# Decay attention and two expert layers in fp32: right-side tiles at multiples of 64 bytes, block sums on VectorE and spread over items, tiles r and hh elsewhere

## Chip, cores, metric

The kernel runs on one core of a Trainium2 chip. The metric is the device time in microseconds (us) of one execution; lower is better. The kernel before took 885.96 us, the median of three runs (884.93 to 888.58).

## What is computed

```python
scores = (q @ k.T) / 8 + minimum(-(cum[i] - cum[j]), 0)   # causal; cum = cumsum(max(s, 0))
x = softmax(scores) @ v                   # 4 batches, 8 heads, 576 tokens, 64 wide -> x [2304, 512]
h = maximum(x @ w_in, 0)                  # w_in [512, 2048]
x = (h * h) @ w_out                       # w_out [2048, 512]
h = maximum(x @ w1, x @ w2, x @ w3)       # each [512, 768]
out = h @ w_out2                          # [768, 512]
```

All is float32 (the weights come as 64-bit numbers whose bits the kernel takes apart). A matrix product is made of three matmuls on pairs of float32r tiles, a high part and a low part: high by high, high by low, low by high.

## The kernel before, in words

The program has three stages, one behind the other on TensorE (PE). Every engine works through its own queue in the order in which the program was written; the kernel is recorded with a manual schedule, so nothing reorders it.

**Attention** goes over 16 head pairs in 9 units each. Its last steps scale an output tile `ax` by reciprocal row sums `px` on GpSimd (`w_px`, line 795) and store it to `x_at` in HBM (`w_xst`, line 800). The first products of the next stage (`first_products`) are already made between its last units.

**Stage 1** is the first expert layer, in nine visits of token chunks: the three chunks of 512 and one of 384 tokens with the first 8 of 16 feature blocks, the last chunk of 384 with all 16, then the four again with the last 8. An item is one block: 12 matmuls `h` (line 813, moving operand `xs`), then on ScalarE (ACT) relu (line 976), square (977) and the high copy into `hh` (978), on VectorE (DVE) the low part (979), and two items later 12 matmuls `x` (line 999) that stream `hh` as the moving operand into four accumulating PSUM banks. Weights stand in slots `sl` of 4 KB in each partition, 15 of them in the first visit and 19 later, and one more, `slb`, on the right side. The class `Slots` decides what is loaded, made (lines 398 to 439) or fetched back, and evicts the weight whose next use is farthest.

**Stage 2** is the second layer: three groups of 768 tokens, 9 items in each, 7 products of 6 matmuls in each item (line 1139; a block algorithm with 7 products in place of 8). Its operands are sums and differences of four raw tiles `xr` of the input, each split into high and low parts in a tile `xs` by `operand` (ACT line 805, DVE line 808); four of the seven operands need a difference first, made in place by GpSimd (line 928). The results are joined on DVE by `after` (lines 1058, 1075, 1080) into `res`, `split_out` splits `res` into `hh`, and 18 matmuls (line 1111) make each 128 output tokens. In the queue of PE the products of item n and those of item n-1 take turns: (n,0), (n-1,4), (n,1), (n-1,5), (n,2), (n-1,6), (n,3). All operands of the next group are made while a group's last item, number 8, runs:

```python
if m % PER == PER - 1 and g < last:
    ops.pop((g, i))
    operand(g + 1, i)
```

SBUF is handed out from two ends. Left are the slots, the attention's tiles, and `xs`, `xr`; right are the staging tiles `st`, `wa`, `slb` and the tiles `hh`, `r`, `sums`, `hi`, `pt` of stage 1. In the built program every right-side tile of stage 1 starts 32 bytes past a multiple of 64 (`hh` at 190,432, `r` at 164,832), and the left-side ones at a multiple of 64. The two buffers of `r` lie on bytes that `ax` and `px` of the attention used.

Of the kernel before, what the change touches and what calls it, by code (L numbers as in the profile page):

```python
# [17 lines left out]
SLOTS_B = 1  # L18
# [20 lines left out]
RETIRE = 16  # L39
QUIET = 0  # L40
PACE_EARLY = 1.5
# [47 lines left out]
class Slots:  # L89
# [8 lines left out]
    def __init__(self, steps, make, bring, early, room, parts):  # L98
        self.steps = steps
        self.uses = {}  # L100
        for n, ids in enumerate(steps):
            for i in ids:
                self.uses.setdefault(i, []).append(n)
        self.make, self.bring, self.early, self.room = make, bring, early, dict(room)
        self.parts = parts
        self.free = []
        self.retired = []
        self.held = {}
        self.open = []
        self.kept = set()  # L110
        self.coming = set()
        self.pos = 0
        self.clock = 0.0
        self.last = -100.0
        self.pace = PACE_ATT
        self.phase = 0
        self.soon_kept = SOON_KEPT
        self.most = ADV_ATT
        self.idle = ()
        self.quiet = set()  # L120
# [13 lines left out]
    def evict(self, n):  # L134
        busy = [job.i for job in self.open]
        while True:
            far = max((j for j in self.held if j not in busy), key=self.next_use)
            if self.next_use(far) <= n:
                return False
            t = self.held.pop(far)  # L140
            if not any(t is r for r in self.retired):
                self.free.append(t)
                return True

    def retire(self, tiles):
        self.retired = tiles
        self.free = [t for t in self.free if not any(t is r for r in tiles)]
# [104 lines left out]
def kernel(  # L252
# [57 lines left out]
    phS = ExitStack()  # L310
    stage_p = phS.enter_context(tc.tile_pool(name="stage", bufs=ST_BUFS, side="right"))
    slots_b = phS.enter_context(tc.tile_pool(name="slb", bufs=1, side="right"))
    slots_b = [slots_b.tile([P, 2, 512], F32R, name=f"slb{i}") for i in range(SLOTS_B)]

# [210 lines left out]
    slots.add(slots_a[:-HELD_BACK] + slots_b)  # L525
# [358 lines left out]
    def experts():  # L884
        xs_p = ctx.enter_context(tc.tile_pool(name="xs", bufs=8, reuse_waits="tile"))
        xr_p = ctx.enter_context(tc.tile_pool(name="xr", bufs=4, reuse_waits="tile"))
# [36 lines left out]

        def operand(g, i):
            a, b, c, d = (raw[g, k] for k in range(4))
            sub = {1: (a, b, a), 2: (a, d, a), 4: (b, d, b), 6: (a, c, a)}.get(i)
            if sub:
                nc.gpsimd.tensor_tensor(out=sub[0], in0=sub[1], in1=sub[2], op=ALU.subtract)  # L928
            x = {3: c, 4: b, 5: d}.get(i, a).rearrange("p (k c) -> p k c", c=T2)
            t = ops[g, i] = xs_p.tile([P, 2, 2, T2], F32R, tag="xs", name="xs")  # L930
            high(x, t[:, :, 0, :])
            low_of(x, t[:, :, 0, :], t[:, :, 1, :])

        with ExitStack() as ph1:
            h_p, sp, r_p, pt_p = (ph1.enter_context(tc.tile_pool(name=n, bufs=b, side="right", reuse_waits="tile"))
                                  for n, b in (("hh1", 4), ("spare", 1), ("rr1", RR), ("part", 4)))
# [9 lines left out]
            for kind, v, m, f in main1:  # L946
# [4 lines left out]
                if kind == "h":  # L951
# [9 lines left out]
                    if nxt:  # L961
                        for kk in range(KD):
                            if to_end == 7 - kk:
                                xload(v + 1, *nxt, kk)
                    elif to_end in (7, 6):
                        for i in range(2):
                            raw_load(0, 2 * (7 - to_end) + i)
                    if end:
                        for kk in (2, 3):
                            if nxt:  # L970
                                xs[v + 1, kk] = xsplit(v + 1, nxt[1], kk)
                            else:
                                operand(0, kk)
# [8 lines left out]
                    if to_end in (5, 3):  # L982
# [3 lines left out]
                        else:  # L986
                            operand(0, kk)
# [4 lines left out]
                else:  # L992
                    w = slots.get(("out", f))
                    hh = hs.pop((v, m))
                    for d in range(KD):
# [5 lines left out]
                        if end:  # L1001
# [9 lines left out]
                            nc.sync.dma_start(out=(part if v < last1 else x_mid)[d, :, t0:t0 + n], in_=dst)  # L1011
                slots.pos += 1
                if slots.pos == len(main1) - RETIRE:
                    slots.retire(slots_b)
                slots.pump(n / 512)
            for i in range(4, 7):
                operand(0, i)
# [5 lines left out]
        for i in [i for i, t in slots.held.items() if any(t is b for b in slots_b)]:  # L1023
            del slots.held[i]
        phS.close()
        slots.soon_kept = SOON_KEPT_2
        with ExitStack() as ph2:
            r_p, hh_p, c_p, s_p, o_p = (ph2.enter_context(tc.tile_pool(name=n, bufs=2, reuse_waits="tile"))
                                        for n in ("rr2", "hh2", "cc2", "ss2", "oo2"))
# [95 lines left out]
            for item in main2:  # L1125
                if item[0] == "p":
# [16 lines left out]
                    if m % PER == PER - 1 and g < last:  # L1143
                        ops.pop((g, i))
                        operand(g + 1, i)
                    if m % PER == PER - 1 and i == 6 and g < last:
                        split_out(g, 0, range(NQ))
                    if m == len(items) - 1 and i == 5:
                        for t in range(2):
                            split_out(last, t, order2[:-1])  # L1150
# [74 lines left out]
```

## Time and profile before

| | before |
|---|---|
| median of 3 runs | 885.96 us (884.93 to 888.58) |
| profiled execution, its own time | 887.15 us |
| its span, first to last instruction | 885.4 us |
| PE busy | 842.1 us (95%), 5284 matmuls |
| DVE busy | 536.0 us (61%) |
| ACT busy | 409.7 us (46%) |
| GpSimd (POOL) busy | 180.9 us (20%) |
| granted TensorE clock, mean | 0.992 of full |

The profile is of one execution. Its page gives busy time by engine, the chain of waits that ended last, and groups of instructions by line. "PEclk" is the granted TensorE clock as a share of the full 2.4 GHz; the lower level is 1.2 GHz, 0.5. A busy PE is not a PE at its peak: matmuls overlap, so how fast it goes is read from the starts of rows that follow each other.

### The profile page before, as it was taken

The numbers are of one execution on the slowest core, as the hardware profiler recorded it, in microseconds if no ns is written. First come the engines' busy times: TensorE is split into PE (matmuls) and PEld (weight loads), VectorE is DVE, ScalarE is ACT, GpSimd is POOL, SyncE is SP. The second block draws the span as 40 slices with busy tenths as digits, with TensorE's granted clock in tenths as the row PEclk, the third lists the DMA queues.
The fourth block names the chain that finished last, engine by engine and source line by source line (L and its number), as shares of the span: only waits on it lengthen the run. The fifth ranks groups of instructions, "written<-read, shape, count | busy, mean of one in ns | idle before, by whom it ended". The sixth has DMA issues, their size and how long they took to land.

```text
span 885.4 us, 14354 instructions
## 1 busy us (share of the span) xinstructions
PE 842.1 (95%) x5284; PEld 708.0 (80%) x5284; DVE 536.0 (61%) x1047; ACT 409.7 (46%) x831; POOL 180.9 (20%) x245
## 2 busy tenths in 40 slices
PE   5899899889999999999999999999989999899998
PEld 3555555458888889999998888889988899789986
DVE  6788787938675556656678686644364343733342
ACT  5788878854444444445444544442242212321212
POOL 2042333334111222213123232220030001200000
PEclk9999999999999999999999999999999999999999
DMA  4555567534244654796559586639911572026501
GB/s 136 169 159 173 166 186 196 171 124 142 79 161 136 205 183 144 285 363 225 199 179 312 174 295 227 236 132 405 378 48 42 200 261 92 13 72 227 200 1 71
DMA packets 71925, 158.70 MB, mean 179 GB/s; under 512 B 11312, under 2 KB 31344, under 8 KB 71856
## 3 DMA queue, kind: packets, MB, share of 16 engines
q1 hardware_dynamic: 56916, 107.45, 35.8%
q0 software_dynamic: 14928, 50.34, 16.6%
q8 instruction: 41, 0.67, 0.3%
q14 instruction: 28, 0.23, 0.1%
q10 hardware_dynamic: 12, 0.01, 0.0%
HBM read 112.48 MB, written 45.27 MB: 178 GB/s over the span
## 4 chain that ended last, share of the span: by engine, by line
PE 83%; DVE 7%; ACT 4%; DMA 2%; issue 2%; POOL 1%; SPq 0%; ACTq 0%; DVEq 0%; POOLq 0%
PE banks L999 23%; PE banks L813 11%; PE first L813 11%; PE banks L1139 11%; PE banks L1111 9%; PE first L1139 7%; PE pairs L782 4%; PE pairs L730 3%; PE pair L648 2%; PE pairs L648 2%; DVE e L671 1%; DVE xs L808 1%; ACT et L759 1%; ACT et L757 1%; ACT e L685 1%
## 5 line engine op out<-in xcount | busy, mean ns | idle before, releaser
L999 PE MATMUL banks<-hh,sl 128*128 128x512 f32 (+1 forms) x900 | 203.8, 376 | 2.6 <-ACT hh L978 2.6
L999 PEld LDWEIGHTS banks<-hh,sl 128*128 128x128 f32 x900 | 166.3, 189 | 28.1 <-ACT hh L978 3.0
L1139 PE MATMUL banks<-xs,sl 128*128 128x384 f32 x702 | 133.5, 339 | 4.1 <-DVE c L1058 4.1
L1139 PEld LDWEIGHTS banks<-xs,sl 128*128 128x128 f32 x702 | 124.6, 191 | 5.7 <-DVE c L1058 4.8
L979 DVE TENSOR_TENSOR hh<-r,hh 128x512 fp32r<-128x512 f32 (+1 forms) x80 | 52.3, 653 | 121.6 <-ACT hh L978 121.4
L813 PE MATMUL first<-xs,sl 128*128 128x512 f32 (+1 forms) x432 | 94.7, 368 | 0.0
L813 PE MATMUL banks<-xs,sl 128*128 128x512 f32 (+1 forms) x432 | 94.7, 368 | 0.0
L1139 PE MATMUL first<-xs,sl 128*128 128x384 f32 x432 | 86.1, 338 | 2.9 <-DVE xs L808 2.4
L685 ACT ACTIVATE e<-e,nm 128x128 f32<-128x128 f32 (+2 forms) x144 | 83.4, 582 | 11.3 <-DVE nm L671 11.2
L813 PEld LDWEIGHTS first<-xs,sl 128*128 128x128 f32 x432 | 79.0, 188 | 10.4
L813 PEld LDWEIGHTS banks<-xs,sl 128*128 128x128 f32 x432 | 79.0, 188 | 10.4
L1111 PE MATMUL banks<-sl,hh 128*128 128x512 f32 (+1 forms) x342 | 80.3, 388 | 4.1 <-DVE hh L808 3.7
L1139 PEld LDWEIGHTS first<-xs,sl 128*128 128x128 f32 x432 | 76.6, 190 | 4.2 <-DVE xs L808 3.0
L1111 PEld LDWEIGHTS banks<-sl,hh 128*128 128x128 f32 x342 | 62.4, 191 | 19.0 <-DVE hh L808 6.0
L976 ACT ACTIVATE r<-first 128x512 f32<-128x512 f32 (+1 forms) x40 | 22.2, 556 | 109.9 <-PE first L813 101.6
L976 ACT ACTIVATE r<-banks 128x512 f32<-128x512 f32 (+1 forms) x40 | 22.2, 556 | 92.5 <-PE banks L813 92.5
L730 PEld LDWEIGHTS pairs<-identF,e 64*128 64x128 f32 x800 | 33.5, 139 | 30.8 <-ACT et L759 23.2
L928 POOL TENSOR_TENSOR xr<-xr 128x768 f32<-128x768 f32 x12 | 24.9, 2088 | 162.1 <-DVE xs L808 162.1
L730 PE MATMUL pairs<-identF,e 64*128 64x64 f32 x800 | 41.4, 231 | 17.0 <-ACT et L759 17.0
L1040 ACT COPY s<-first 128x384 f32<-128x384 f32 x36 | 17.2, 479 | 79.5 <-PE first L1139 79.3
L782 PEld LDWEIGHTS pairs<-et,xv 128*64 128x64 f32 (+1 forms) x448 | 27.8, 136 | 31.2 <-ACT e L685 8.9
L782 PE MATMUL pairs<-et,xv 128*64 128x320 f32 (+4 forms) x448 | 52.7, 367 | 0.0
(108 smaller groups left out, 1200.4 us busy)
## 6 DMA issues: line engine op xcount, KB each, us to landing
sl<-keep_p SPq DMA_DIRECT2D x68, 512.0 KB
st<-in_w_dram POOLq DMA_DIRECT2D x36, 256.0 KB, 5.7
st<-in_w_out_dram POOLq DMA_DIRECT2D x35, 256.0 KB, 4.1
sl<-keep_out SPq DMA_DIRECT2D x14, 512.0 KB
keep_p<-hi POOLq DMA_DIRECT2D x9, 768.0 KB, 4.8
keep_p<-sums POOLq DMA_DIRECT2D x9, 768.0 KB, 6.2
xr<-x_at SPq DMA_DIRECT2D x20, 256.0 KB
xk<-in_kT_dram SPq DMA_DIRECT2D x16, 288.0 KB
```

The source lines that it names most:

```text
L648: nc.tensor.matmul(b[:, j, 0:w], lhsT=d["xq"][rows(j), w - P:w], rhs=d["xk"][rows(j), 0:w], start=True, stop=False)
L685: nc.scalar.activation(out=e_u[u][:, 0:w], in_=e_u[u][:, 0:w], func=ACTF.Exp, scale=-1.0, bias=st.pop(n), accum_out=sums[p, win][:, col:co ...
L730: nc.tensor.transpose(t[:, h, at * D:(at + 1) * D], e_u[v][rows(h), k * P:(k + 1) * P], identF[rows(h), rows(h)])
L782: nc.tensor.matmul(pv[rows(j), f:(W0, W1)[w]], lhsT=xv[0:kr, j, k, :], rhs=rhs, start=(k == 0), stop=(k == last))
L813: nc.tensor.matmul(hps[:, 0:n], lhsT=w[:, wp, kk * P:(kk + 1) * P], rhs=x[kk][xp][:, 0:n], start=(kk == 0 and c == 0), stop=(kk == KD - 1 ...
L928: nc.gpsimd.tensor_tensor(out=sub[0], in0=sub[1], in1=sub[2], op=ALU.subtract)
L976: nc.scalar.activation(out=r[:, 0:n], in_=hps[:, 0:n], func=ACTF.Relu)
L979: nc.vector.tensor_tensor(out=hh[:, 1, 0:n], in0=r[:, 0:n], in1=f32(hh[:, 0, 0:n]), op=ALU.subtract)
L999: nc.tensor.matmul(xacc[d][:, 0:n], lhsT=w[:, wp, d * P:(d + 1) * P], rhs=hh[:, xp, 0:n], start=(m == 0 and c == 0), stop=(end and c == 2))
L1040: nc.scalar.copy(out=x, in_=bank[:, 0:T2])
L1111: nc.tensor.matmul(b, lhsT=hh[g, t][:, hp_, q, h, :], rhs=w[:, wp, lo:hi], start=(begin and n == h == c == 0), stop=(end and n == len(f) - ...
L1139: nc.tensor.matmul(at[m, b][:, 0:T2], lhsT=w[:, wp, at_w + kk * P:at_w + (kk + 1) * P], rhs=x[:, kk, xp, :], start=(i in (0, 1, 3) and kk ...
```

## The change

Five edits:

1. A pool `pad` of 96 bytes is put at the right end, ahead of the staging tiles, so that every right-side tile starts at a multiple of 64 bytes (`hh` at 194,432, `r` at 190,336).
2. The slot `slb` goes, with the code that retired it; stage 1 has one slot fewer in each visit.
3. In stage 1 the pools are opened in another order, `hh`, `r`, `spare`, `part`, so that `r` no longer lies on bytes of the attention.
4. The differences go from GpSimd to DVE (`raw_sub`), one of them into a fifth `xr` tile, and differences and operands follow two tables: for group 0 over the last items of stage 1, for the other groups over items 4 to 8 of the group before. The pool `cc2` goes from two buffers to one for room.
5. In the last group the split of the first two blocks of `res` for the first two output tiles goes from the last item to the one before.

Line numbers of the changed file are 6 to 9 lower at the same statements.

```diff
-SLOTS_B = 1
...
-RETIRE = 16
+FIRST_OPS = {6: ((1, 1), (0, 0)), 5: ((1, 4), (1, 2)), 4: ((0, 1),), 3: ((1, 6), (0, 2)), 2: ((0, 3),)}
+NEXT_OPS = {(4, 1): ((1, 1),), (5, 1): ((0, 0),), (6, 1): ((1, 4),), (7, 1): ((1, 2),), (8, 0): ((0, 1),), (8, 1): ((1, 6), (0, 2)),
+            (8, 2): ((0, 3),), (8, 3): ((0, 4),), (8, 4): ((0, 5),), (8, 5): ((0, 6),)}
...
+    phS.enter_context(tc.tile_pool(name="pad", bufs=1, side="right")).tile([P, 24], F32, name="pad")
     stage_p = phS.enter_context(tc.tile_pool(name="stage", bufs=ST_BUFS, side="right"))
-    slots_b = phS.enter_context(tc.tile_pool(name="slb", bufs=1, side="right"))
-    slots_b = [slots_b.tile([P, 2, 512], F32R, name=f"slb{i}") for i in range(SLOTS_B)]
...
-    slots.add(slots_a[:-HELD_BACK] + slots_b)
+    slots.add(slots_a[:-HELD_BACK])
...
-        xr_p = ctx.enter_context(tc.tile_pool(name="xr", bufs=4, reuse_waits="tile"))
+        xr_p = ctx.enter_context(tc.tile_pool(name="xr", bufs=5, reuse_waits="tile"))
...
+        def raw_sub(g, i):
+            if i == 1:
+                raw[g, 4] = xr_p.tile([P, 2 * T2], F32, tag="xr", name="xr")
+            out, x, y = {1: (4, 1, 0), 2: (0, 3, 4), 4: (1, 3, 1), 6: (4, 2, 0)}[i]
+            nc.vector.tensor_tensor(out=raw[g, out], in0=raw[g, x], in1=raw[g, y], op=ALU.subtract)
+
         def operand(g, i):
-            a, b, c, d = (raw[g, k] for k in range(4))
-            sub = {1: (a, b, a), 2: (a, d, a), 4: (b, d, b), 6: (a, c, a)}.get(i)
-            if sub:
-                nc.gpsimd.tensor_tensor(out=sub[0], in0=sub[1], in1=sub[2], op=ALU.subtract)
-            x = {3: c, 4: b, 5: d}.get(i, a).rearrange("p (k c) -> p k c", c=T2)
+            x = raw[g, {1: 4, 3: 2, 4: 1, 5: 3, 6: 4}.get(i, 0)].rearrange("p (k c) -> p k c", c=T2)
...
-            h_p, sp, r_p, pt_p = (ph1.enter_context(tc.tile_pool(name=n, bufs=b, side="right", reuse_waits="tile"))
-                                  for n, b in (("hh1", 4), ("spare", 1), ("rr1", RR), ("part", 4)))
+            h_p, r_p, sp, pt_p = (ph1.enter_context(tc.tile_pool(name=n, bufs=b, side="right", reuse_waits="tile"))
+                                  for n, b in (("hh1", 4), ("rr1", RR), ("spare", 1), ("part", 4)))
...
+                    if not nxt:
+                        for f_, i in FIRST_OPS.get(to_end, ()):
+                            (raw_sub if f_ else operand)(0, i)
...
-                    if m % PER == PER - 1 and g < last:
-                        ops.pop((g, i))
-                        operand(g + 1, i)
+                    if g < last:
+                        for f_, k in NEXT_OPS.get((m % PER, i), ()):
+                            (raw_sub if f_ else operand)(g + 1, k)
                     if m % PER == PER - 1 and i == 6 and g < last:
                         split_out(g, 0, range(NQ))
-                    if m == len(items) - 1 and i == 5:
-                        for t in range(2):
-                            split_out(last, t, order2[:-1])
+                    if m == len(items) - 2 and i in (1, 4):
+                        split_out(last, i // 4, order2[:-1])
```

A key (m, i) of `NEXT_OPS` stands for product i of item m, behind which the step is written; (1, k) is `raw_sub` k, (0, k) is `operand` k.

The queue of ACT at the start of stage 1, with the semaphores that each instruction waits for (`first` and `banks` are PSUM banks). Before:

```order
L762 COPY et_2829<-pairs_90 128x2x5x64 [waits DVE_49]
L976 ACTIVATE r<-first_2839 128x512 [waits DMAHW3_49,DMAHW4_49,DMAHW2_49,DMAHW5_49,DMAHW1_49,DMAHW6_49,DMAHW0_49,DMAHW7_49,PE_49,Pool_49]
L977 ACTIVATE r<-r 128x512 [waits Activation_49]
L978 CAST hh<-r 128x512 [waits Activation_49]
L435 CAST sl_77<-wa 128x512
```

Now:

```order
L756 COPY et_2829<-pairs_90 128x2x5x64 [waits DVE_49]
L970 ACTIVATE r<-first_2839 128x512 [waits PE_49]
L971 ACTIVATE r<-r 128x512 [waits Activation_49]
L972 CAST hh<-r 128x512 [waits Activation_49]
L429 CAST sl_77<-wa 128x512 [waits Pool_49]
```

The first relu of stage 1 no longer waits for GpSimd and for eight DMA semaphores, only for its product on PE.

The queue of DVE at the end of group 0, from behind the second operand of group 1 to the split of `res` for the first output tile. Before:

```order
L808 TENSOR_TENSOR xs<-xr,xs 128x2x384
L1080 TENSOR_TENSOR res<-first_2840,res 128x384
L1058 TENSOR_TENSOR c<-banks_2949,s_6784 128x384
L808 TENSOR_TENSOR xs<-xr,xs 128x2x384
L1058 TENSOR_TENSOR c<-banks_2946,s_6804 128x384
L808 TENSOR_TENSOR xs<-xr,xs 128x2x384
L1058 TENSOR_TENSOR c<-banks_2947,s_6826 128x384
L1075 TENSOR_TENSOR res<-res,c 128x1152
L808 TENSOR_TENSOR xs<-xr,xs 128x2x384
L1080 TENSOR_TENSOR res<-banks_2946,res 128x384
L808 TENSOR_TENSOR xs<-xr,xs 128x2x384
L808 TENSOR_TENSOR hh<-res,hh 128x768
```

Now:

```order
L922 TENSOR_TENSOR xr<-xr 128x768
L802 TENSOR_TENSOR xs<-xr,xs 128x2x384
L1050 TENSOR_TENSOR c<-banks_2948,s_6790 128x384
L1067 TENSOR_TENSOR res<-res,c 128x1152
L802 TENSOR_TENSOR xs<-xr,xs 128x2x384
L1072 TENSOR_TENSOR res<-first_2840,res 128x384
L1050 TENSOR_TENSOR c<-banks_2949,s_6814 128x384
L802 TENSOR_TENSOR xs<-xr,xs 128x2x384
L1050 TENSOR_TENSOR c<-banks_2946,s_6834 128x384
L802 TENSOR_TENSOR xs<-xr,xs 128x2x384
L1050 TENSOR_TENSOR c<-banks_2947,s_6856 128x384
L1067 TENSOR_TENSOR res<-res,c 128x1152
```

Each operand's low part stands one product earlier than before, and the three other differences and the first operand stand farther ahead, among the work of items 4 to 7. Behind the last row there follow one `xs`, one `res` and the `hh`.

The queue of DVE in the last two items. Before:

```order
L1058 TENSOR_TENSOR c<-banks_2947,s_8167 128x384
L1075 TENSOR_TENSOR res<-res,c 128x1152
L808 TENSOR_TENSOR hh<-res,hh 128x256 x4
L1080 TENSOR_TENSOR res<-banks_2946,res 128x384
L808 TENSOR_TENSOR hh<-res,hh 128x256 x2
```

Now:

```order
L1050 TENSOR_TENSOR res<-first_2839,s_8066 128x384
L802 TENSOR_TENSOR hh<-res,hh 128x256 x2
L1050 TENSOR_TENSOR res<-banks_2947,s_8084 128x384
L1050 TENSOR_TENSOR c<-banks_2949,s_8107 128x384
L1050 TENSOR_TENSOR c<-first_2840,s_8122 128x384
L802 TENSOR_TENSOR hh<-res,hh 128x256 x2
```

The four splits that stood behind the last item's wide maximum now stand in two pairs among the sums of the item before.

## Rows read from the trace of the kernel before

**Rows 1.** Windows: us; busy us (instructions) of PE, PEld, DVE, ACT, POOL; PEclk, DMA, GB/s.

```profile
190.00:200.00 10.00, 7.36 (x24) 5.24 (x24) 3.48 (x7) 6.38 (x11) 4.61 (x6) 0.83 0.60 196
200.00:590.00 390.00, 390.00 (x1868) 341.56 (x1867) 259.84 (x434) 186.27 (x316) 104.60 (x170) 1.00 0.58 202
...
655.00:670.00 15.00, 11.11 (x50) 9.74 (x49) 14.59 (x14) 6.52 (x10) 6.09 (x3) 0.89 0.00 0
...
755.00:770.00 15.00, 11.24 (x47) 9.19 (x46) 11.73 (x13) 5.03 (x9) 3.23 (x2) 0.89 0.00 1
...
850.00:860.00 10.00, 7.79 (x30) 6.28 (x29) 4.45 (x9) 0.51 (x2) 0.00 (x0) 0.83 0.01 2
```

**Rows 2.** Timeline of PE, 180 to 196: start, length, instruction, count, [idle before, releaser].

```profile
183.74 3.48 PE L813 MATMUL first<-sl,sl 128*128 128x512 f32 x14
...
189.49 3.03 PE L813 MATMUL banks<-sl,sl 128*128 128x512 f32 x12
195.11 1.52 PE L999 MATMUL banks<-hh,sl 128*128 128x512 f32 x2 [2.58 <-ACT hh L978]
```

**Rows 3.** Timeline of ACT, 184 to 196.

```profile
193.15 0.60 ACT L976 ACTIVATE r<-first 128x512 f32<-128x512 f32 x1 [8.30 <-POOL ax L795]
```

**Rows 4.** Chain of waits, 184 to 196: start, length, what.

```profile
191.20 1.69 DMA x_at<-ax
```

**Rows 5.** Timeline of PE, 655 to 670.

```profile
660.13 1.14 PE L1139 MATMUL first<-xs,sl 128*128 128x384 f32 x5 [1.21 <-DVE xs L808]
663.33 3.73 PE L1139 MATMUL banks<-xs,sl 128*128 128x384 f32 x12 [2.05 <-DVE c L1058]
```

**Rows 6.** Timeline of DVE, 653 to 669.

```profile
654.93 2.63 DVE L1075 TENSOR_TENSOR res<-res,c 128x1152 f32<-128x1152 f32 x1
...
664.64 1.36 DVE L1075 TENSOR_TENSOR res<-res,c 128x1152 f32<-128x1152 f32 x1
665.91 0.95 DVE L808 TENSOR_TENSOR xs<-xr,xs 128x768 fp32r<-128x768 f32 x1
666.78 0.55 DVE L1080 TENSOR_TENSOR res<-banks,res 128x384 f32<-128x384 f32 x1
...
668.24 0.96 DVE L808 TENSOR_TENSOR hh<-res,hh 128x768 fp32r<-128x768 f32 x1
```

**Rows 7.** Groups by line and form: busy us, mean ns | idle before, releasers.

```profile
L928 POOL TENSOR_TENSOR xr<-xr 128x768 f32<-128x768 f32 x12 | 24.9, 2088 | 162.1 <-DVE xs L808 162.1
L1040 ACT COPY s<-first 128x384 f32<-128x384 f32 x36 | 17.2, 479 | 79.5 <-PE first L1139 79.3
L805 ACT CAST hh<-res 128x768 fp32r<-128x768 f32 x16 | 13.4, 837 | 11.8 <-DVE res L1080 9.0 <-PE banks L1111 2.7
```

**Rows 8.** Chain of waits, 600 to 610.

```profile
604.67 1.04 PE first L1139 x6
```

**Rows 9.** Timeline of PE, 205 to 218, and 402 to 409.

```profile
208.12 2.98 PE L999 MATMUL banks<-hh,sl 128*128 128x512 f32 x12
210.94 2.92 PE L813 MATMUL first<-sl,sl 128*128 128x512 f32 x12
213.69 2.98 PE L999 MATMUL banks<-hh,sl 128*128 128x512 f32 x12
...
402.46 2.27 PE L813 MATMUL first<-xs,sl 128*128 128x384 f32 x12
404.57 2.28 PE L999 MATMUL banks<-hh,sl 128*128 128x384 f32 x12
406.69 2.27 PE L813 MATMUL first<-xs,sl 128*128 128x384 f32 x12
```

**Rows 10.** Timeline of PE, 846 to 870.

```profile
853.44 4.38 PE L1111 MATMUL banks<-sl,hh 128*128 128x512 f32 x11 [2.21 <-DVE hh L808]
```

**Rows 11.** Timeline of DVE at 222 and of PE at 224.

```profile
222.02 0.69 DVE L439 TENSOR_TENSOR sl<-wa,sl 128x512 fp32r<-128x512 f32 x1
...
224.84 2.98 PE L999 MATMUL banks<-hh,sl 128*128 128x512 f32 x12
```

More of the change, by code (lines that the diff above doesn't have):

```diff
@@ L106, in __init__ @@
         self.free = []
-        self.retired = []
         self.held = {}
@@ L140, in evict @@
             t = self.held.pop(far)
[L141 to L147, printed above, removed]
+            self.free.append(t)
+            return True
     def fill(self, i):
@@ L964, in experts @@
                                 xload(v + 1, *nxt, kk)
-                    elif to_end in (7, 6):
-                        for i in range(2):
-                            raw_load(0, 2 * (7 - to_end) + i)
+                    elif to_end == 7:
+                        for i in range(4):
+                            raw_load(0, i)
                     if end:
@@ L971, in experts @@
                                 xs[v + 1, kk] = xsplit(v + 1, nxt[1], kk)
-                            else:
-                                operand(0, kk)
                     r = r_p.tile([P, 512], F32, tag="r", name="r")
@@ L985, in experts @@
                             xs[v + 1, kk] = xsplit(v + 1, nxt[1], kk)
-                        else:
-                            operand(0, kk)
+                    if not nxt:
+                        for f_, i in FIRST_OPS.get(to_end, ()):
+                            (raw_sub if f_ else operand)(0, i)
                     if v > last1 and m == LAG:
@@ L1011, in experts @@
                             nc.sync.dma_start(out=(part if v < last1 else x_mid)[d, :, t0:t0 + n], in_=dst)
+                    if not nxt and m >= len(fs) - 2:
+                        for i in ((5, 6) if end else (4,)):
+                            operand(0, i)
                 slots.pos += 1
-                if slots.pos == len(main1) - RETIRE:
-                    slots.retire(slots_b)
                 slots.pump(n / 512)
-            for i in range(4, 7):
-                operand(0, i)
             for i in made2 + late:
@@ L1022, in experts @@
                     slots.finish(i)
-        for i in [i for i, t in slots.held.items() if any(t is b for b in slots_b)]:
-            del slots.held[i]
         phS.close()
@@ L1027, in experts @@
         with ExitStack() as ph2:
-            r_p, hh_p, c_p, s_p, o_p = (ph2.enter_context(tc.tile_pool(name=n, bufs=2, reuse_waits="tile"))
-                                        for n in ("rr2", "hh2", "cc2", "ss2", "oo2"))
+            r_p, hh_p, c_p, s_p, o_p = (ph2.enter_context(tc.tile_pool(name=n, bufs=b, reuse_waits="tile"))
+                                        for n, b in (("rr2", 2), ("hh2", 2), ("cc2", 1), ("ss2", 2), ("oo2", 2)))
             rings = dict(X=Ring(banks[0:3]), Z=Ring(banks[3:5]), Y=Ring(banks[5:6]))
```

## Prediction

> **What bounds the kernel now.** The busy times come first: PE is busy 842.1 of 885.4 us, 95%, DVE 61%, ACT 46%. So a gain must come from the stretches in which PE stands still or goes slowly. The second view is the windows [rows 1]. A window's loss is its length less PE's busy time, plus what the granted clock lacks: (1 - PEclk) x length. From 200 to 590 PE is busy for all of 390.00 us at clock 1.00: there no wait counts, only the pace of the matmuls. Four windows lose: 190 to 200 has 2.64 idle + 1.70 clock = 4.34 us; 655 to 670, 3.89 + 1.65 = 5.54; 755 to 770, 3.76 + 1.65 = 5.41; 850 to 860, 2.21 + 1.70 = 3.91. The clock's share is the wait's own follow-up: PE stands still and the granted clock then averages 0.83 to 0.89, so part of the window ran at 1.2 GHz instead of 2.4. Who ends each wait is read from the timelines of the engines there.
>
> At 195 PE waits 2.58 us for the first `hh` [rows 2]. ACT idled 8.30 us ahead of the relu that begins this `hh`, and the releaser is POOL's `ax` [rows 3]; the store of `ax` ran from 191.20 to 192.89 [rows 4], and the relu began at 193.15. Its product on PE lies in a row that ended at 183.74 + 3.48 = 187.22 at the latest [rows 2]. So the relu waited for its tile `r`, which lies on the bytes of `ax`, not for data.
>
> At 663 PE waits 2.05 us for DVE's `c`, and 1.21 before that for an `xs` [rows 5]. DVE is full: 14.59 of 15.00 us [rows 1]. Four of the seven operands need POOL's difference (2.09 us mean [rows 7]), then ACT's high copy (0.84 [rows 7]), then DVE's low part (0.95 [rows 6]), in series. A wide maximum costs 2.63 us while POOL works and 1.36 later [rows 6].
>
> At 853 the 18 output matmuls wait 2.21 us for `hh` [rows 10], whose four low parts on DVE stand behind the last item's wide maximum.
>
> **The change, part by part.**
>
> *Pools in another order (start of stage 1).* The first relu waits only for PE. It can begin when its product is done, by 187.2 instead of 193.15, six us earlier, and PE's wait is 2.58. The whole 4.34 goes. Bounds: 0 (another wait) to 4.34. I take **-4.3**.
>
> *Right-side tiles at multiples of 64.* The matmuls of L999 stream `hh`, which sits 32 bytes past a multiple of 64; those of L813 stream tiles that sit on one. Both have 12 matmuls of 512 columns per item. From start to start, L999 takes 210.94 - 208.12 = 2.82 us and L813 213.69 - 210.94 = 2.75 [rows 9]: 0.07, and 0.065 as the mean over the stretch, which I use. There are 48 such items (3 chunks x 16 blocks), and PE is saturated there, so each one counts in full: 48 x 0.065 = 3.1. For the 32 items of 384 columns L999 takes 406.69 - 404.57 = 2.12, and twice six products of stage 2, from a tile on a multiple of 64, 2 x 1.04 = 2.08 [rows 8, 9]; but L813's item just before takes 404.57 - 402.46 = 2.11, and as the nearest row it makes me take nothing. Bounds: 0, since L999 also differs in going through four banks, and 48 x 0.07 + 32 x 0.04 = 4.6. The nearest row is L813's at the same form: **-3.1**. A page of the Trainium skill speaks against this term: "SBUF — State Buffer", section "Operand start alignment", says that an operand need only start at a multiple of its element size (and that this is about legality, not speed), and its section "Specifications (TRN2)" gives cachelines of 16 bytes, and `hh` starts on one of these before and after; by these the term would be nothing. That is the first rival.
>
> *Differences on DVE, spread.* POOL loses 12 x 2.09 = 25 us; DVE gains 12 subtractions of 128 x 768. DVE shows no such subtraction; the low part is one, of the same shape, with one output type less: 0.95 us, 0.87 from start to start [rows 6]. That is 12 x 0.95 = 11.4 us in all. Those of group 0 stand in the last items of stage 1, where DVE is busy 259.84 of 390 [rows 1] and PE does not wait; those of the other groups, except one, stand in items 4 to 7: at DVE's 61% they are hidden. If that cover were gone, each would cost up to 0.95. What is left at a boundary goes by DVE's queue. From the end of product (8,0) to the next group's first product, PE has 14 products x 1.04 = 14.56 us [rows 8]. In that time DVE must do 6 low parts, 1 difference, 5 sums of 384, 2 wide maxima and 2 small ones. Start to start [rows 6] these take 6 x 0.87 + 0.87 + 5 x 0.47 + 2 x 1.27 + 2 x 0.47 = 11.9; at full durations 6 x 0.95 + 0.95 + 5 x 0.55 + 2 x 1.36 + 2 x 0.55 = 13.2. It begins 1.4 later (ACT's copy 0.48 and high copy 0.84 [rows 7], and the hops) and ends with a high copy and a low part, 1.8. So the chain is 15.1 to 16.4, and PE's wait 0.6 to 1.9. I take 1.3, the middle, without a fall of the clock. Each boundary then gives 5.54 - 1.3 = 4.24 and 5.41 - 1.3 = 4.11: **-8.35**. Bounds: at least 1.9 + 1.65 = 3.55 is left at each (then 3.85 for both), at most nothing (10.95).
>
> *Splits of the last group an item earlier.* The four low parts now stand among the sums of the item before, whose seven products give PE 7 x 1.04 = 7.3 us to cover them. The 2.21 us and the clock behind it go: **-3.9**; bounds 0 to 3.91. What is late next is the last block's split at 864, which already follows now.
>
> *At nothing.* `slb` goes: in the first visit 15 places are left of 16, and two weights of `w_in` are made once more, six or seven items before use. That adds 2 x 0.69 us on DVE [rows 11], four half loads on POOL, which has just lost 25 us, and two casts on ACT; all lie beside a saturated PE. `cc2` with one buffer makes a sum wait for the maximum that reads `c`, but both are on DVE, in this order. The four raw loads of group 0 go out in one item instead of two, an item earlier on SP for two of them; nothing waits there. The count of matmuls is the same.
>
> Sum: -4.3 - 3.1 - 8.35 - 3.9 = -19.7. The profiled execution took 887.15, 1.75 more than its span and 1.2 more than the median of 885.96. It becomes 867.4, and the median 866.3, which rounds to 866.
>
> **Rivals.**
>
> R1, *the address of `hh` doesn't matter.* L999's 0.07 us would come from its banks, which change with every output block, and stay. For it: L999 and L813 differ in that too. Against: at 384 columns the banks change as well, and the two are alike. 866.3 + 3.1 = 869.4.
>
> R2, *DVE becomes the bound at the boundaries.* The chain is as long as at full durations, PE waits 1.9 twice, and the clock falls as it does now, 1.65. For it: DVE has 14.59 of 15.00 [rows 1] and its work there gets less only by what moves to items 4 to 7. Against: POOL is silent there, so maxima take 1.36 rather than 2.63 [rows 6]. 866.3 + 2 x (3.55 - 1.3) = 870.8.
>
> R3, *the start's wait is replaced* by the next thing that the first `hh` needs, a weight or the tile under `hh`. 866.3 + 4.3 = 870.6.
>
> R4, *slower.* With one place less and PE 4.3 us earlier, the weights of the first visits come late: load on POOL's queue, cast on ACT, low part on DVE, then the product. The weight of 222.02 + 0.69 = 222.71 is used from 224.84 on [rows 11]: 2.1 us of room. From a start that is earlier by more than that, weights that don't move with it are late. In the first two visits up to six are made so close. At the price of the start's wait, 2.58 + 1.70 = 4.28 each, that is 25.7: 866.3 + 25.7 = 892.0. Against: each weight is begun by a place in the queues, which moves with PE, and POOL, ACT and DVE are busy only 27 to 67% there [rows 1].
>
> **How the numbers follow.** Forecast 0.52, R1 0.20, R2 0.13, R3 0.10, R4 0.03, anything else 0.02. The likeliest gives 866. The range: down, the forecast with the upper bounds, 4.6 for the alignment (-1.5) and nothing left at the boundaries (-2.6), is 862.2; up, R1 to R3 each give at most 870.8, and R1 with R2 873.9, of which I take half of the step: 862 to 873. About 0.5% is what a measurement of this kernel can tell from no change, 4.4 us: faster is below 881.5, slower above 890.4. R1 to R3 stay below 881.5; only R4 lies above 890.4. So faster 0.95, same 0.02, slower 0.03.
>
> **What would show it.** *Start:* the relu's wait names PE and PE's 2.58 us is gone, at clock 1.00 in the first 10 us of the stage; wrong if another releaser ends a wait there. *Alignment:* twelve L999 matmuls of 512 columns from start to start at 2.75 rather than 2.82; wrong if 2.82. *Boundaries:* no POOL differences, the last wait 0.6 to 1.9 us and PEclk near 1.00; wrong if the wait is 2 us or more, ended by DVE's low parts or maxima, with the clock at 0.89. *End:* the 2.21 us ahead of the output matmuls gone. *Weights:* PE busy throughout stage 1; wrong if waits on `sl` come up in the first two visits. A time above 873 says that two terms fail together, one below 862 that matmuls elsewhere got faster too.

## The result, and the profile after

The changed kernel took 861.56 us, the median of four runs (859.52 to 863.2), against 885.89: a ratio of 0.9719 (0.969 to 0.9749), 24.3 us less. Its profiled execution took 859.52, its span 857.7. The forecast was 866, the range 862 to 873: the way was right, and the time 0.4 us below the range.

The windows after, at the stretches that answer to those of before [rows 1] (the places lie earlier now):

```profile
190.00:200.00 10.00, 10.00 (x46) 8.28 (x45) 4.89 (x9) 4.95 (x8) 5.36 (x6) 1.00 0.78 246
200.00:575.00 375.00, 375.00 (x1836) 333.24 (x1835) 265.18 (x445) 184.80 (x314) 97.74 (x169) 1.00 0.60 211
640.00:655.00 15.00, 14.43 (x76) 13.08 (x75) 10.20 (x14) 5.93 (x9) 0.00 (x0) 1.00 0.00 0
735.00:750.00 15.00, 14.43 (x76) 13.06 (x75) 8.58 (x12) 5.75 (x9) 0.00 (x0) 1.00 0.05 18
825.00:835.00 10.00, 10.00 (x50) 8.78 (x50) 4.35 (x7) 0.71 (x2) 0.00 (x0) 1.00 0.01 2
```

The four losses of 4.34, 5.54, 5.41 and 3.91 us are now 0, 0.57, 0.57 and 0, and the clock no longer falls in any of them. That is 18.1 us.

PE in two stretches of stage 1, to be read from start to start [rows 9]:

```profile
206.87 2.88 PE L994 MATMUL banks<-hh,sl 128*128 128x512 f32 x12
209.59 2.88 PE L807 MATMUL banks<-sl,sl 128*128 128x512 f32 x12
212.31 2.88 PE L994 MATMUL banks<-hh,sl 128*128 128x512 f32 x12
...
396.31 2.24 PE L807 MATMUL first<-xs,sl 128*128 128x384 f32 x12
398.39 2.24 PE L994 MATMUL banks<-hh,sl 128*128 128x384 f32 x12
400.47 1.72 PE L807 MATMUL banks<-xs,sl 128*128 128x384 f32 x9
```

Twelve matmuls of 512 columns take 2.72 us on *both* lines, where before it was 2.82 on the one that streams `hh` and 2.75 on the other; with 384 columns both take 2.08, before 2.12 and 2.11. PE was and is busy without a break there, so no busy share shows this: only the starts do. It is the term that I had at 3.1 us.

### The profile page after: what moved, and what is told of

Read it like the earlier page. It is cut to its first block, busy times and chain, and to the rows that moved or that the text cites. A ratio compares the mean times of both kernels' runs of the same rounds, so it can differ in the third digit from the quotient of the medians.

```text
span 857.7 us, 14355 instructions
## 1 busy us (share of the span) xinstructions
PE 826.3 (96%) x5284; PEld 701.0 (82%) x5284; DVE 541.7 (63%) x1071; ACT 411.2 (48%) x833; POOL 159.9 (19%) x237
## 4 chain that ended last, share of the span: by engine, by line
PE 89%; DVE 4%; ACT 3%; DMA 3%; issue 1%; SPq 0%; ACTq 0%; DVEq 0%
PE banks L994 23%; PE banks L1131 13%; PE first L807 12%; PE banks L807 12%; PE banks L1103 9%; PE first L1131 8%; PE pairs L776 4%; PE pairs L724 3%; PE pairs L642 2%; PE pair L642 2%; ACT et L753 1%; DMA xv<-in_v_tail_dram 1%; DVE e L665 1%; ACT e L679 1%; DMA sl<-keep_p 1%
## 5 line engine op out<-in xcount | busy, mean ns | idle before, releaser
L994 PE MATMUL banks<-hh,sl 128*128 128x512 f32 (+1 forms) x960 | 209.9, 367 | 0.0
L994 PEld LDWEIGHTS banks<-hh,sl 128*128 128x128 f32 x960 | 175.1, 188 | 22.6
L1131 PE MATMUL banks<-xs,sl 128*128 128x384 f32 x702 | 131.2, 335 | 0.0
L1131 PEld LDWEIGHTS banks<-xs,sl 128*128 128x128 f32 x702 | 122.8, 188 | 0.9 <-DMA sl<-keep_p 0.2
L807 PEld LDWEIGHTS banks<-xs,sl 128*128 128x128 f32 x432 | 78.6, 188 | 9.4
L1103 PE MATMUL banks<-sl,hh 128*128 128x512 f32 (+1 forms) x342 | 78.4, 382 | 1.9 <-DVE hh L802 1.5
L1032 ACT COPY s<-banks 128x384 f32<-128x384 f32 x45 | 21.6, 480 | 58.4 <-PE banks L1131 57.9
```

The lines of the kernel that those rows point to most:

```text
L807: nc.tensor.matmul(hps[:, 0:n], lhsT=w[:, wp, kk * P:(kk + 1) * P], rhs=x[kk][xp][:, 0:n], start=(kk == 0 and c == 0), stop=(kk == KD - 1 ...
L994: nc.tensor.matmul(xacc[d][:, 0:n], lhsT=w[:, wp, d * P:(d + 1) * P], rhs=hh[:, xp, 0:n], start=(m == 0 and c == 0), stop=(end and c == 2))
L1032: nc.scalar.copy(out=x, in_=bank[:, 0:T2])
L1103: nc.tensor.matmul(b, lhsT=hh[g, t][:, hp_, q, h, :], rhs=w[:, wp, lo:hi], start=(begin and n == h == c == 0), stop=(end and n == len(f) - ...
L1131: nc.tensor.matmul(at[m, b][:, 0:T2], lhsT=w[:, wp, at_w + kk * P:at_w + (kk + 1) * P], rhs=x[:, kk, xp, :], start=(i in (0, 1, 3) and kk ...
```

## The experiments

Two readings are used below. The **pace** is the mean ns from one matmul's start to the next, by line and form (the number of columns), over the whole trace, steps across a wait left out. The **stretch** is the time from the first matmul that streams `hh` to the end of the last one; it leaves out the attention before it, whose end lies anywhere from 187.4 to 192.7 us in the profiles of these runs though its code is the same, and so moves the medians by some us. In the kernel before the stretch is 396.2 us (1.7 of it the slow clock at its start), in the changed one 386.6. The medians also differ between sets: the kernel before, taken anew beside each set of runs, had medians from 884.8 to 887.9.

**First set: is it the address at all, and whose?**

a1_pad_only, the kernel before with one line more:

```diff
+    phS.enter_context(tc.tile_pool(name="pad", bufs=1, side="right")).tile([P, 24], F32, name="pad")
     stage_p = phS.enter_context(tc.tile_pool(name="stage", bufs=ST_BUFS, side="right"))
```

> The kernel before with the pad alone. Theory A (the address of the right-side tiles is what sped up stage 1): twelve matmuls of 512 columns at 227 ns each from start to start on both lines, instead of 234 (line 999) and 230 (line 813), 384 columns at 173.5; 7.9 us less, some 878. Theory B (only the pace of the matmuls that stream hh depends on it): 4.3 + 1.1 = 5.4 us less, 880.5. Theory C (the gone slot and the other places of the pools did it, the address nothing): spacing and time as before, 886.

876.4 us, ratio 0.9888 (0.9871 to 0.9904), 9.7 less; pace 227 and 173.5 ns on both lines. Theory A. Its profiled span is 10.8 us shorter than that of before: 7.35 lie in the stretch, 1.7 ahead of it (the attention ended 1.6 earlier, which lies within what it varies by), and 1.8 in stage 2.

a2_no_pad, the changed kernel without that line:

> The changed kernel without its pad: all right-side tiles 32 bytes past a multiple of 64 again. Theory A: spacing of before comes back on both lines, 7.9 us more than the changed kernel, some 869.5. Theory B: only the line that streams hh goes back to 234 ns, 5.4 more, 867. Theory C: 861.6, unchanged.

868.55 us, pace 234.5 and 229.8 ns, the stretch 394.5: 7.9 more than with the pad (the medians are 7.0 apart). So the address makes 7.9 us, and C falls, for the slot and the order of the pools are the new ones here. B falls as well: the line that does not stream `hh` pays too.

a3_hh_only and a4_all_but_hh (the latter without the pad at the right end as well). `right` opens one pool; the pools stand in the changed kernel's order, with two pads between them:

```diff
+            right("padhh1", 1).tile([P, 8], F32, name="padhh1")
             h_p = right("hh1", 4)
+            right("padrr1", 1).tile([P, 8], F32, name="padrr1")
             r_p = right("rr1", RR)
```

> The changed kernel with only the four hh tiles of stage 1 moved to 32 bytes past a multiple of 64. Theory A1 (TensorE's moving operand is what minds its start): the line that streams hh at 234 ns, the other at 227; 5.4 us more, 867. Theory A2 (other engines' reads and writes at such addresses take SBUF time from TensorE): both lines slower, the one that does not stream hh too, by part of its 3 ns; time between 863 and 869.5.

> The changed kernel with all right-side tiles but hh at 32 bytes past a multiple of 64 (staging, r, partial sums, weight sums). Theory A1: all spacing at 227 and 173.5 ns, 861.6. Theory A2: 3 ns per matmul of 512 columns and 2 of 384 on both lines, 3 to 5 us more, some 866.

a3: 867.02 us, pace 233.5 and 228.7. a4: 865.2, pace 230.2 and 230.6. Both lines are slow in both, as A2 has it. But within an item the spacing repeats to the ns (standard deviation 0 to 2 over 43 items), while work of VectorE, GpSimd and the DMAs falls on it now here, now there; that doesn't look like a port that is fought over. And in a4 `hh` had moved as well, to 64 past a multiple of 128. So this pair decided nothing, and the second set put each address where it can be told apart.

**Second set.** b1_hh_64 moves `hh` down by 64 bytes and what lies below it by 128, all at multiples of 64. b2_others_32 leaves `hh` on its very bytes and puts the rest 32 past a multiple of 64:

```diff
 b1:
+            right("padhh1", 1).tile([P, 16], F32, name="padhh1")
             h_p = right("hh1", 4)
+            right("padrr1", 1).tile([P, 16], F32, name="padrr1")
 b2 (without the pad at the right end):
+            right("padhh1", 1).tile([P, 24], F32, name="padhh1")
             h_p = right("hh1", 4)
+            right("padrr1", 1).tile([P, 8], F32, name="padrr1")
```

> The changed kernel with only the tiles from hh on moved down by 64 bytes: all right-side tiles still at a multiple of 64, hh no longer at a multiple of 128. Theory A1 in its new form (only where TensorE's moving operand starts counts, and a multiple of 64 is not enough): the spacing of the run with all but hh at 32 past, whose hh stood here too: 230 ns on both lines, some 865. Theory A2 (other engines' accesses at 32 past a multiple of 64): 227 on both lines, 861.6.

> The changed kernel with hh at the very bytes it has there (194,432), and staging, r, partial sums and weight sums at 32 past a multiple of 64. Theory A1: 227 and 173.5 ns on both lines, 861.6. Theory A2: both lines slower by 3 ns at 512 columns, 3 to 5 us more, some 866.

The timelines of PE from 230 us, first of b1, then of b2:

```profile
230.37 2.96 PE L1001 MATMUL banks<-hh,sl 128*128 128x512 f32 x12
233.17 2.90 PE L807 MATMUL banks<-xs,sl 128*128 128x512 f32 x12
235.91 2.96 PE L1001 MATMUL banks<-hh,sl 128*128 128x512 f32 x12
```

```profile
231.02 2.88 PE L806 MATMUL banks<-xs,sl 128*128 128x512 f32 x12
233.74 2.88 PE L1000 MATMUL banks<-hh,sl 128*128 128x512 f32 x12
236.46 2.88 PE L806 MATMUL banks<-xs,sl 128*128 128x512 f32 x12
```

b1 takes 2.80 and 2.74 (866.23 us), b2 2.72 and 2.72 (860.64 us, the stretch 386.6). A2 is out: with staging, `r` and the sums 32 bytes past a multiple of 64 the pace is that of the changed kernel. And the change's own description, multiples of 64, is not the rule: b1 keeps it and is slow.

c4_xs_64 asks whether this is `hh`'s own affair, by moving `xs` and stage 2's tiles instead:

```diff
+        ctx.enter_context(tc.tile_pool(name="padx", bufs=1)).tile([P, 16], F32, name="padx")
         xs_p = ctx.enter_context(tc.tile_pool(name="xs", bufs=8, reuse_waits="tile"))
```

> The changed kernel with 64 bytes ahead of the tiles xs on the left, which puts the moving operand of line 807 (and of stage 2's products) at 64 past a multiple of 128, hh untouched. Theory A1 (any moving operand is slower that does not start at a multiple of 128): line 807 at 233 ns for 512 columns in the 40 of 48 items that stream xs, 3.1 us, and 0.6 in the matmuls of line 994 behind them, some 865; 384 columns as now, 173 to 174, as they were with hh at 64. Rival (it is hh's own affair, since ACT and VectorE write it just before): 227 ns, 861.6.

866.04 us. The line that streams `xs` went to 229.8 ns and the line of `hh` behind it to 229.9, though `hh` and its weights lay as in the changed kernel. The output products slowed down as well, and they stream *weights*, which had not moved, past `hh` of stage 2, which had. PE in group 0's output, first the changed kernel, then c4:

```profile
675.69 4.28 PE L1103 MATMUL banks<-sl,hh 128*128 128x512 f32 x18
679.81 1.23 PE L1131 MATMUL banks<-xs,sl 128*128 128x384 f32 x6
```

```profile
670.93 4.36 PE L1104 MATMUL banks<-sl,hh 128*128 128x512 f32 x18
675.13 3.29 PE L1132 MATMUL banks<-xs,sl 128*128 128x384 f32 x18
```

4.12 against 4.20 us for 18, or from 228.7 to 233.1 ns. So a tile that is loaded as the *weights* of a matmul counts as much as one that is streamed. That left two rules: each must start well, or both must start alike.

**Third set: absolute or relative.** d1_hh_128 moves `hh` down by 128 bytes; d2_all_64 is b1 with all of the left side, weights and `xs`, moved up by 64; d3_left_64 is the changed kernel with that alone:

```diff
 d1:
+            right("padhh1", 1).tile([P, 32], F32, name="padhh1")
             h_p = right("hh1", 4)
+            right("padrr1", 1).tile([P, 32], F32, name="padrr1")
 d2 and d3:
+    perm.tile([P, 16], F32, name="padp")
     slots_a = [perm.tile([P, 2, 512], F32R, name=f"sl{i}") for i in range(SLOTS_A)]
```

> The changed kernel with hh moved down by 128 bytes, to a multiple of 256, where the weights and xs stand at 128 past one. If a multiple of 128 is what counts: 227 and 173.5 ns on both lines, 861.6. If the streamed tile and the weights must stand alike modulo 256: over 229 ns on the line that streams hh, some 864.

> The changed kernel with everything that TensorE reads in stages 1 and 2 moved by 64 bytes: weights, xs and hh all at 64 past a multiple of 128. If each operand's own start counts: 230 to 234 ns for 512 columns on both lines and on the output products, 8 us more, some 870. If only the distance between streamed tile and weights counts: 227 ns, 861.6.

> The changed kernel with the left side moved by 64 bytes (weights, xs, stage 2's tiles) and hh of stage 1 left at a multiple of 128. If each operand's own start counts: the line that streams xs is slow in itself (231 to 234 ns), and so are the output products. If the distance counts: the line that streams xs, whose weights have moved with it, shows 227 ns but for the first few behind the slow line that streams hh (233); output products as in the changed kernel.

The built program gives where tiles start: `hh` at 194,432 in the changed kernel, the weights from 16,512 in steps of 4,096, `xs` at 94,336. With the distance, the start of the streamed tile `hh` less that of the weights, modulo 256, all runs fall into line (pace in ns):

| distance mod 256 | runs | streams hh, 512 | 384 | other line, 512 | stretch, us |
|---|---|---|---|---|---|
| 0 | changed; b2 | 226.8; 226.8 | 173.5; 173.5 | 227.0; 227.1 | 386.60; 386.59 |
| 64 | a4 | 230.2 | 172.9 | 230.6 | 391.05 |
| 96 | a2 (and before) | 234.5 (234.4) | 176.5 (176.4) | 229.8 (229.9) | 394.51 |
| 128 | d1; d2 | 232.7; 232.7 | 176.3; 176.3 | 228.0; 228.1 | 391.67; 391.67 |
| 192 | b1; d3 | 233.3; 233.3 | 173.2; 173.2 | 228.4; 228.4 | 391.24; 391.24 |
| 224 | a3 | 233.5 | 174.3 | 228.7 | 392.44 |

d1 and d2 have `hh` and the weights at different places but the same distance, and their stretches agree to 0.01 us; so do b1 and d3. It is the distance. c4 agrees: its `xs` stands at distance 64 and takes 230.2 ns with 512 columns and 173.0 with 384, as `hh` does in a4, and its output products, whose streamed weights stand at 192 from `hh`, take 233.1, as the line of `hh` does in b1 and d3. In d3 the line of `xs`, whose weights moved with it, shows 227 ns from its sixth matmul on and is slow only in those right behind an item of `hh`; by absolute starts it would have been slow throughout. The times, 864.22 (d1), 867.39 (d2) and 863.71 (d3), are of two runs each and hold the attention's part.

The trace of before held this, and I passed it by. The slot `slb` lay exactly 16,384 bytes above the first `hh`, so the items with weights there had distance 0:

```profile
233.23 2.92 PE L813 MATMUL first<-xs,sl 128*128 128x512 f32 x12
235.99 2.94 PE L999 MATMUL banks<-hh,slb 128*128 128x512 f32 x12
238.77 2.92 PE L813 MATMUL banks<-xs,sl 128*128 128x512 f32 x12
```

2.78 us with `slb`, 2.82 with the others [rows 9]; at 384 columns 174.0 ns against 176.5.

**The other parts.** b3_pad_order is a1 with the pools in the new order:

```diff
-            h_p, sp, r_p, pt_p = (...
-                                  for n, b in (("hh1", 4), ("spare", 1), ("rr1", RR), ("part", 4)))
+            h_p, r_p, sp, pt_p = (...
+                                  for n, b in (("hh1", 4), ("rr1", RR), ("spare", 1), ("part", 4)))
```

> The kernel before with the pad and with the pools in the order hh, r, spare, part. If the relu's wait for the tile r was all that held the start of stage 1: 4.3 us less than the pad alone (876.4), 872.1, and no wait over 0.3 us ahead of the first product of hh. Rival R3 (another wait takes its place): 876.4, with another releaser in the row.

874.01 us. PE at the start of stage 1, a1 and then b3:

```profile
187.87 3.03 PE L814 MATMUL banks<-sl,sl 128*128 128x512 f32 x12
193.42 0.50 PE L1000 MATMUL banks<-hh,sl 128*128 128x512 f32 x1 [2.51 <-ACT hh L979]
```

```profile
188.82 3.03 PE L814 MATMUL banks<-sl,sl 128*128 128x512 f32 x12
191.69 2.88 PE L1000 MATMUL banks<-hh,sl 128*128 128x512 f32 x12
```

The wait of 2.51 is gone, and nothing took its place. From the end of the attention to the end of the stretch a1 has 394.3 us and b3 389.4, 4.9 less, the price forecast plus some. The medians differ by 2.4 only: in the profiles b3's attention ended 1.0 later and its stage 2 took 1.4 more. Each against the kernel before of its own set, a1 is 9.7 us less and b3 13.9, which is 4.2 apart.

b4_late_split puts the last group's split back:

```diff
-                    if m == len(items) - 2 and i in (1, 4):
-                        split_out(last, i // 4, order2[:-1])
+                    if m == len(items) - 1 and i == 5:
+                        for t in range(2):
+                            split_out(last, t, order2[:-1])
```

> The changed kernel with the last group's splits put back into the last item. If they cost what the windows showed (2.2 us of wait and 1.7 of clock): 3.9 us more than the changed kernel, 865.5. Rival (the wait was DVE being late for other reasons, which the other edits removed): 861.6.

864.83 us, 3.3 more. In the profiles its stage 2 is 3.0 longer, though a wait at the start of stage 2 is 1.0 shorter: 4.0 for the splits. Its timeline of PE, with a wait as long as the one before [rows 10]:

```profile
831.24 4.00 PE L1103 MATMUL banks<-sl,hh 128*128 128x512 f32 x11 [2.21 <-DVE hh L802]
```

c1_pool_sub and c2_item8 take the differences apart: the engine, and the spreading.

```diff
 c1:
-            nc.vector.tensor_tensor(out=raw[g, out], in0=raw[g, x], in1=raw[g, y], op=ALU.subtract)
+            nc.gpsimd.tensor_tensor(out=raw[g, out], in0=raw[g, x], in1=raw[g, y], op=ALU.subtract)
 c2:
+NEXT_OPS = {(8, 0): ((0, 0),), (8, 1): ((1, 1), (0, 1)), (8, 2): ((1, 2), (0, 2)), (8, 3): ((0, 3),),
+            (8, 4): ((1, 4), (0, 4)), (8, 5): ((0, 5),), (8, 6): ((1, 6), (0, 6))}
```

> The changed kernel with the twelve differences on GpSimd, at their new places. Theory D (spreading them over items is what freed the boundaries): within 1 us of the changed kernel, 862, the waits at the boundaries about 1 us as there. Theory E (it was the engine: GpSimd's 2.09 us in the chain, and the maxima of 2.63 beside it): the waits and the clock of before come back at both boundaries, 4.5 us each, some 870.

> The changed kernel with differences on VectorE but all of groups 1 and 2 written, like their operands, in the last item of the group before. Theory D: VectorE has 3 differences and 1 low part more in that item, 4 x 0.87 = 3.5 us, and gets late by as much: a wait of 4 us and 1.65 of clock in place of 0.9 at each boundary, 9.5 in all, some 871. Theory E: 862, as the changed kernel.

c1: 861.69 us, no different from the changed kernel; stage 2 takes 277.1 us in it and 277.2 there. A wait for a DMA at its start is 1.1 shorter in c1 (0.40 against 1.52 us), so the differences on GpSimd cost stage 2 about 1.0; 0.93 us is idle at each boundary, against 0.57. The window at its first boundary:

```profile
640.00:665.00 25.00, 24.07 (x126) 21.99 (x125) 13.42 (x19) 8.66 (x14) 0.00 (x0) 1.00 0.06 22
```

c2: 877.61, 16 more. PE at the first boundary and the windows at both, of c2:

```profile
649.18 2.37 PE L1131 MATMUL banks<-xs,sl 128*128 128x384 f32 x12 [0.82 <-DVE c L1050]
651.39 1.21 PE L1131 MATMUL first<-xs,sl 128*128 128x384 f32 x6
657.56 0.75 PE L1103 MATMUL banks<-sl,hh 128*128 128x512 f32 x1 [4.96 <-ACT hh L799]
658.68 6.85 PE L1103 MATMUL banks<-sl,hh 128*128 128x512 f32 x17 [0.38 <-DVE hh L802]
```

```profile
645.00:665.00 20.00, 13.84 (x54) 11.22 (x54) 11.37 (x15) 6.21 (x10) 0.00 (x0) 0.83 0.00 0
745.00:765.00 20.00, 13.88 (x59) 11.49 (x58) 12.16 (x16) 6.21 (x10) 0.00 (x0) 0.83 0.00 0
```

So it is the spreading that freed the boundaries, and the engine hardly matters once they are spread. Moved to VectorE without spreading, the differences make each boundary lose 6.1 us idle and 3.4 of clock, more than before. I had 4 and 1.65: I had counted VectorE's work but not its waits, 0.9 us for ACT's high copy after each of four differences:

```profile
654.96 0.95 DVE L922 TENSOR_TENSOR xr<-xr 128x768 f32<-128x768 f32 x1
656.80 0.96 DVE L802 TENSOR_TENSOR xs<-xr,xs 128x768 fp32r<-128x768 f32 x1 [0.90 <-ACT xs L799]
657.68 0.95 DVE L802 TENSOR_TENSOR hh<-res,hh 128x768 fp32r<-128x768 f32 x1
```

c3_early_split goes on where the changed kernel still waits, 0.57 us at each boundary:

```diff
-                    if m % PER == PER - 1 and i == 6 and g < last:
-                        split_out(g, 0, range(NQ))
+                    if g < last and (m % PER, i) in ((PER - 2, 1), (PER - 1, 6)):
+                        done = [items[PER * g + 3 * k][1] for k in range(NQ)]
+                        split_out(g, 0, done[-1:] if i == 6 else done[:-1])
```

> The changed kernel with the split for the first output tile of groups 0 and 1 cut as in the last group: two blocks in item 7, the last block behind product 6 of item 8. If the 0.33 and 0.81 us that TensorE waits there for hh come from the 0.84 + 0.96 us of the split of three blocks: 1.1 us less at each of two boundaries, 859.4. Rival: another wait takes the place (the new group's bank, or VectorE's own queue), 861.6.

The rows at the first boundary, of the changed kernel and of c3:

```profile
648.61 1.21 PE L1131 MATMUL first<-xs,sl 128*128 128x384 f32 x6
649.89 0.50 PE L1103 MATMUL banks<-sl,hh 128*128 128x512 f32 x1
650.88 4.17 PE L1103 MATMUL banks<-sl,hh 128*128 128x512 f32 x17 [0.49 <-DVE hh L802]
654.89 1.23 PE L1131 MATMUL first<-xs,sl 128*128 128x384 f32 x6
```

```profile
652.88 1.20 PE L1131 MATMUL first<-xs,sl 128*128 128x384 f32 x6
653.92 4.28 PE L1103 MATMUL banks<-sl,hh 128*128 128x512 f32 x18
658.04 1.23 PE L1131 MATMUL first<-xs,sl 128*128 128x384 f32 x6
```

The wait is gone, and stage 2 takes 274.5 us instead of 277.2; 0.66 of the 2.7 are a shorter wait for a DMA at its start, so 2.0 is the split's. That is more than the 2 x 0.57 of idle: between its two waits PE runs one matmul, which counts as busy for 0.50 us. From the six products ahead of the output tile to the six behind it the changed kernel takes 654.89 - 648.61 = 6.28 us and c3 658.04 - 652.88 = 5.16. So a boundary still cost about 1.0 us. In the time, 861.23 (857.28 to 861.83, five runs), it can't be told from the changed kernel's 861.56: the attention of its profiled run alone ended 4.9 us later. It is the better by its own stretch; that the whole kernel is faster isn't shown.

## Why the prediction was right, and where it failed

- **Start, -4.3: right.** The window lost 4.34 and loses nothing; the first relu, ahead of which ACT idled 8.30 us [rows 3], begins without a wait. R3 is out (b3).

```profile
182.96 0.60 ACT L970 ACTIVATE r<-first 128x512 f32<-128x512 f32 x1
```

- **End, -3.9: right**, by the window and by b4 (+3.3 in the time, 4.0 in stage 2).
- **Boundaries, -8.35: right in kind, short in size.** In the windows 0.57 is left at each, not 1.3; the gain, counted in the same way as the forecast, is 9.8. That the 0.57 meets the lower bound of 0.6 is in part luck: VectorE's 16 operations take 12.4 us in the rows below, from 636.53 to the end of the one at 648.42, between the 11.9 and 13.2 of the forecast, and by c3 a boundary still loses about 1.0, of which the window shows only the idle part. R2 did not come, but c2 shows that it is near: the same work in one item costs 9.5 us at each boundary. As a cause, "differences on VectorE" was worth about 1.0 us of stage 2 (c1); what worked was their place.

```profile
636.53 0.96 DVE L802 TENSOR_TENSOR xs<-xr,xs 128x768 fp32r<-128x768 f32 x1 [1.67 <-ACT xs L799]
...
648.42 0.55 DVE L1072 TENSOR_TENSOR res<-banks,res 128x384 f32<-128x384 f32 x1
649.87 0.96 DVE L802 TENSOR_TENSOR hh<-res,hh 128x768 fp32r<-128x768 f32 x1 [0.90 <-ACT hh L799]
```

- **Alignment, -3.1: this step failed.** It measured 7.9 (a2). I took line 813's 2.75 us as the pace of a matmul whose tiles start well, and line 813 was slow itself, because the first matmuls behind an item of `hh` are slow too: by the trace of before the last four of its 12 run at 226 to 227 ns, the eight ahead of them at 225 to 235. The same line made me put 384 columns at nothing, and the upper bound of 4.6 rests on it too. (The step between the two lines, 0.065 in the forecast, is 0.056 by all items of the trace; that alone would have made the term smaller still, 2.7.) The pace without the fault was in the trace of before, in stage 2: the last nine of the 18 output matmuls (line 1111) that stand together run at 226.7 ns in the mean, and the products of 384 columns at 174. Against that pace of 226.8 to 227.0 and 173.5, both lines paid: 48 x 12 x (7.6 + 2.9 ns) + 32 x 12 x (2.9 + 1.9) = 7.9. The forecast's own sign for a time below 862, matmuls elsewhere faster too, came true on the line that streams `xs`. The reason given was wrong as well as the size: a multiple of 64 is not what counts (b1 keeps it and is slow), and that the pad of 96 bytes brought the distance to a multiple of 256 was luck. R1 is out: with the banks as they were, the pace changes with the start. By the rule of the Trainium skill's page "SBUF — State Buffer", section "Operand start alignment", set beside the term, it would have been nothing; the measured 7.9 us decides, and the page does say that its rule is on legality, not speed.
- **R4, late weights: did not come.** PE is busy for all of 375.00 us, clock 1.00, with one slot fewer.

The four windows give 18.1, the address 7.9, together 26.0 of the 27.7 us between the two spans; the rest, 1.8, is the attention's earlier end. Two smaller things cancel in this sum: a wait for a DMA at the start of stage 2 that is 1.0 longer now, and what the boundaries gave beyond their windows. The medians differ by 24.3: the execution shown of before lay 1.3 above its median, the one after 2.0 below. With 7.9 and 9.8 in place of 3.1 and 8.35 the sum would have been 25.9 and the time 860.1; the measured 861.56 is 1.5 above, less than the 5 us over which the attention's end varies. In the range, half of the step from 870.8 to 873.9 gives 872.4, not 873; the miss lies at the other end.

## What to carry to other kernels

When PE is busy for a whole stage, read its pace from start to start and set each form against the fastest stretch of that form in the whole trace, not against its neighbour. Look at where the streamed tile and the weights start relative to each other: a pad of 96 bytes, which brought that distance to a multiple of 256, was worth 7.9 us here. And when a chain of small steps on three engines stands at a boundary, spread it over the items before; which engine makes a step mattered less than having it made early.

## What the hardware showed that was not expected

The pace of fp32r matmuls depends on the distance, the start of the streamed tile less that of the tile loaded as weights, modulo 256: 512 columns take 227 ns at distance 0 and 230 to 234.5 at the five others tried; 384 columns take 172.9 to 176.5, least at 64. Distance 0 is not best for every form: the 35 matmuls of 256 columns at the end of the kernel take 119.8 ns at 0 and 113.5 at 192 (c4). The slow pace runs on into the next matmuls, up to about ten (the first ten of 12 in c4's line of `hh`), whose own distance is 0. Nor is a bad distance needed for that: in the changed kernel, with every distance at 0, the first nine of 18 output matmuls behind products of 384 columns take 231.3 ns in the mean and the last nine 226.9; why is open. Where each tile starts by itself made no difference (d1 and d2, b1 and d3). That only the remainder by 256 counts, and not the whole distance, rests on a few pairs: at remainder 0, 77,824 for `xs`, a multiple of 4,096, and 177,920 for `hh`, which is none (226.9 and 226.8 ns); at 64, 177,984 for `hh` in a4 and 77,888 for `xs` in c4 (230.2 both); at 192, `hh` in b1 and the output products in c4 (233.3 and 233.1). What in the chip makes it so, no run tells; weights are loaded while columns stream [PEld beside PE in the windows], so two reads that meet would fit, but it is only a guess.
